# Loading one input in longer packets, reordering a kernel's opening, and holding back its weights

## The chip, the cores and the metric

One core of one Trainium2 chip. The metric is the device time of one execution in microseconds (us). Medians and means are over several runs, and every run is listed with the clock that TensorE (PE) was granted on average. A run of this one-core program is labelled "slow" when it is over 1.5% above the fastest run of the same kernel in the same call; verdicts use "fast" runs alone. That label matters here and I come back to it.

## The reference, cut to what matters

A Mamba-2 scan over 4 batches, 8 heads and 768 tokens, then an MLP with a hard-swish between two products:

```
# scan, by chunks
M = (C @ B.T) * exp(cum_i - cum_j) * causal
y = M @ x + (C @ state) * exp(cum_i)
state = exp(sum(la)) * state + sum_j(B_j x_j * exp(cum_last - cum_j))
# MLP on the transposed scan output
h = x @ w_in            # 3072x256 by 256x2048, weights come as float64
g = h * clip(h + 3, 0, 6) / 6
out = g @ w_out
```

## The kernel before

It works in 6 chunks of 128 tokens for all 4 batches. The scan of chunk 0 must be finished before the first product `h` can start. The weights arrive as float64 and are decoded to fp32 on VectorE and ScalarE, in 8 blocks of 1 MB (4 of w_in, 4 of w_out); block 0 is loaded at the start, block 1 is needed at the ninth product of h (the fifth f). The parts that the change touches (cuts are marked):

```
def load_bc(c):
    ...
    if c < TURN:                                    # TURN = 3
        bcs[c] = [tokens_first(C, name="C", tag="bc")]   # one transfer, 64-byte packets
    Bs[c] = tokens_first(B, name="B")
    ...
def load_w(i, hold=False):
    raw = loads.tile([P, NK * FP * 2 * P], U32, name="raw", bufs=NRAW)
    if hold:
        nc.gpsimd.memset(raw[:, :1], 0)             # queued on GpSimd behind ends()
    ...
    nc.sync.dma_start(out=dst, in_=src)

def decode(i):                                      # a generator; weights(i, n) takes n steps
    nc.scalar.copy(out=s, in_=top)
    ...
    if i == 1:
        next(parts_m); next(parts_m)                # significand, two VectorE steps, first
    yield
    # we and ws on VectorE; yield; exponent on ScalarE; yield; exponent again; yield
    # last two VectorE steps: we | ws, then w_in (or w_out) = m * e

# the opening
    diff(0, *range(NB)); store_rows()
    weights(0, 2); diff_exp(0, 0); diff_exp(0, 1); weights(0, 1)
    diff_exp(0, 2); diff_exp(0, 3); weights(0, 1)
    first_eto(); diff(1, 2, 3)
    for b in range(NB):
        ends(0, b)                                  # bs = B * L, on GpSimd
    load_w(1, hold=True); load_w(2); load_w(3)
    t_ps = turn_ps(0, 0)
    turn_c(0, t_ps)                                 # C turned on PE, into PSUM
    diff(1, 0, 1); busy(1, ...); turn_cum(c_ps); weights(0, 1)
    turn_b(0); by_token(c_ps); fade_c(0, t_ps)
    diff_exp(1, 2); diff_exp(1, 3)
    scores(0); multiply(0); renew(0); mix(0); keep(0)
    weights(1, 5)
```

`scores` makes cb = C B^T and the new state's products (y), `multiply` multiplies the decays L by cb in four VectorE steps, `mix` makes y, `keep` copies it out.

## Time and profile before

| | before |
|---|---|
| median (3 runs, then 4) | 365.87 us, then 365.69 us |
| profiled run | 366.87 us, span 365.2 us, mean granted clock 0.986 |
| first h | 27.36 us |
| decode of block 1 starts on VectorE | 27.75 us |
| first o (second product) | 57.25 us |

The profile's lines for this are in the prediction below. To read them: PE and PEld are the matmuls and weight loads of TensorE, DVE is VectorE, ACT ScalarE, POOL GpSimd and SPq the queue of SyncE, which issues the transfers (DMA); "issue" is time in which an engine waited for nothing that the profile shows, and the clock row of the page is in tenths of full speed.

### The profile page before, as it was taken

The numbers are of one execution on the slowest core, as the hardware profiler recorded it, in microseconds if no ns is written. First come the engines' busy times: TensorE is split into PE (matmuls) and PEld (weight loads), VectorE is DVE, ScalarE is ACT, GpSimd is POOL, SyncE is SP. The second block draws the span as 40 slices with busy tenths as digits, with TensorE's granted clock in tenths as the row PEclk, the third lists the DMA queues.
The fourth block names the chain that finished last, engine by engine and source line by source line (L and its number), as shares of the span: only waits on it lengthen the run. The fifth ranks groups of instructions, "written<-read, shape, count | busy, mean of one in ns | idle before, by whom it ended". The sixth has DMA issues, their size and how long they took to land.

```text
span 365.2 us, 9345 instructions
## 1 busy us (share of the span) xinstructions
PE 352.7 (97%) x3938; PEld 302.1 (83%) x3938; DVE 225.1 (62%) x427; ACT 177.0 (48%) x389; POOL 138.5 (38%) x139
## 2 busy tenths in 40 slices
PE   6859999999999999999999999999999999999996
PEld 2644447888788999888999888999888999888996
DVE  6637999989588626488436488436488421488111
ACT  3626887458557380366380366380366110376100
POOL 3300000084188922059922059820057800058800
PEclk9967999999999999999999999999999999999999
DMA  8986959910945016442016442000000000000000
GB/s 162 111 334 165 115 211 174 175 29 31 187 57 75 5 44 135 66 86 23 2 31 148 67 83 25 2 4 31 29 2 1 2 4 31 30 3 0 2 29 31
DMA packets 78538, 24.97 MB, mean 68 GB/s; under 512 B 69088, under 2 KB 74880, under 8 KB 77984
## 3 DMA queue, kind: packets, MB, share of 16 engines
q1 hardware_dynamic: 78496, 24.37, 34.4%
q8 instruction: 31, 0.51, 0.6%
q14 instruction: 11, 0.09, 0.1%
HBM read 21.07 MB, written 3.29 MB: 67 GB/s over the span
## 4 chain that ended last, share of the span: by engine, by line
PE 91%; DVE 4%; issue 2%; ACT 1%; DMA 1%; DVEq 0%; ACTq 0%
PE ob L749 18%; PE even L638 18%; PE oa L749 17%; PE odd L638 13%; PE h L596 8%; PE o L690 8%; PE y L571 3%; PE y L483 2%; PE cb L505 2%; PE y L517 1%; DVE cT L433 1%; PE d L340 1%; PE d L349 1%; ACT even L653 1%; DMA pre<-in_a_dram 1%
## 5 line engine op out<-in xcount | busy, mean ns | idle before, releaser
L735 POOL TENSOR_TENSOR s<-gT 128x512 f32<-128x512 f32 x20 | 26.4, 1321 | 91.4 <-DVE gT L679 91.4
L638 PE MATMUL even<-ts,w_sum 128*128 128x256 f32 x160 | 48.2, 383 | 0.0
L653 ACT COPY even<-odd 128x512 f32<-128x512 f32 x40 | 23.0, 576 | 48.9 <-PE odd L638 46.7
L674 ACT ACTIVATE gT<-odd,half 128x512 f32<-128x512 f32 x40 | 27.5, 687 | 35.0 <-DVE odd L667 35.0
L638 PE MATMUL odd<-yT,w_in 128*128 128x256 f32 x160 | 41.1, 379 | 0.0
L749 PE MATMUL oa<-w_out,gT 128*128 128x128 f32 x320 | 38.9, 277 | 0.0
L749 PEld LDWEIGHTS oa<-w_out,gT 128*128 128x128 f32 x320 | 38.1, 192 | 0.9
L749 PE MATMUL ob<-w_out,s 128*128 128x128 f32 x320 | 37.4, 275 | 0.0
L749 PEld LDWEIGHTS ob<-w_out,s 128*128 128x128 f32 x320 | 36.5, 192 | 0.0
L638 PEld LDWEIGHTS even<-ts,w_sum 128*128 128x128 f32 x160 | 29.9, 190 | 5.3 <-ACT up L660 1.5
L679 DVE SCALAR_TENSOR_TENSOR gT<-gT,odd 128x512 f32<-128x512 f32 x40 | 27.5, 688 | 9.9 <-ACT gT L674 9.9
L638 PEld LDWEIGHTS odd<-yT,w_in 128*128 128x128 f32 x160 | 30.1, 190 | 3.9
L377 ACT ACTIVATE L<-L,cum_n 128x64 f32<-128x64 f32 x128 | 31.1, 335 | 0.0
L749 PE MATMUL ob<-t,gT 128*128 128x128 f32 x240 | 30.3, 279 | 0.0
L596 PE MATMUL h<-yT,w_in 128*128 128x512 f32 x64 | 30.0, 632 | 0.0
L679 DVE SCALAR_TENSOR_TENSOR gT<-gT,even 128x512 f32<-128x512 f32 x40 | 27.2, 679 | 4.4 <-ACT gT L674 4.4
L674 ACT ACTIVATE gT<-even,half 128x512 f32<-128x512 f32 x40 | 27.8, 694 | 4.4 <-PE even L638 4.4
L654 DVE COPY up<-odd 128x256 f32<-128x256 f32 x40 | 17.0, 425 | 19.3 <-ACT even L653 18.6
L749 PEld LDWEIGHTS ob<-t,gT 128*128 128x128 f32 x240 | 27.9, 192 | 1.1 <-issue 0.4
L690 PE MATMUL o<-w_out,gT 128*128 128x256 f32 x128 | 28.5, 381 | 0.0
L395 POOL TENSOR_TENSOR tmp<-state,eto 128x256 f32<-128x256 f32 x5 | 3.2, 637 | 65.0 <-ACT eto L381 64.9
L690 PEld LDWEIGHTS o<-w_out,gT 128*128 128x128 f32 x128 | 24.1, 190 | 3.7 <-issue 0.5
(129 smaller groups left out, 629.7 us busy)
## 6 DMA issues: line engine op xcount, KB each, us to landing
raw<-in_moe_w_in_dram SPq DMA_DIRECT2D x4, 1024.0 KB
raw<-in_moe_w_out_dram SPq DMA_DIRECT2D x4, 1024.0 KB
L<-cum_d SPq DMA_DIRECT2D x8, 512.0 KB
xt<-in_x_dram SPq DMA_DIRECT2D x6, 512.0 KB
out_dram<-res SPq DMA_DIRECT2D x20, 128.0 KB
B<-in_B_dram SPq DMA_DIRECT2D x6, 256.0 KB
eto<-cum_e SPq DMA_DIRECT2D x20, 64.0 KB
C<-in_C_dram SPq DMA_DIRECT2D x3, 256.0 KB
```

The costliest lines, as they stand in the source:

```text
L377: nc.scalar.activation(Ls[c][:, b, h], Ls[c][:, b, h], AF.Exp, bias=cum_n[:, c, g:g + 1])
L483: nc.tensor.matmul(out=ys[c][a, q // 2][d0:d0 + 2 * D, b], lhsT=state[pair, b], rhs=csT[pair, b, HALF[a]], start=(a == 0 and b == 0), stop ...
L571: nc.tensor.matmul(out=ys[c][a, u][d0:d0 + D, b], lhsT=xt[rows, b * NH + h], rhs=Ls[c][rows, b, h], start=(b == 0 and a >= min(c, 1)), sto ...
L596: nc.tensor.matmul(out=h.rearrange("p r i -> p (r i)"), lhsT=w_in[:, j, f * P:(f + 1) * P], rhs=yTs[k][:, j].rearrange("p b i -> p (b i)") ...
L638: nc.tensor.matmul(out=bank[:, r], lhsT=lhsT, rhs=rhs, start=start, stop=True, skip_group_check=True)
L653: nc.scalar.copy(out=even, in_=odd[:, 1:2].to_broadcast([P, 2, 2 * P]))
L654: nc.vector.tensor_copy(out=up[:, 1], in_=odd[:, 0])
L674: nc.scalar.activation(gTs[k][:, f], h.rearrange("p r i -> p (r i)"), AF.Relu, bias=half, scale=1.0 / 6.0)
L679: nc.vector.scalar_tensor_tensor(out=g, in0=g, scalar=1.0, in1=h.rearrange("p r i -> p (r i)"), op0=ALU.min, op1=ALU.mult)
L690: nc.tensor.matmul(out=o[:, b % 2], lhsT=gTs[0][:, f, b * P:(b + 1) * P], rhs=w_out[:, f], start=(f == 0 and b % 2 == 0), stop=True, skip_ ...
L735: nc.gpsimd.tensor_tensor(out=o, in0=p_, in1=q_, op=op)
L749: nc.tensor.matmul(out=bank[:, slot], lhsT=lhs[:, j], rhs=rhs[:, j], start=(clear and j == 0), stop=True, skip_group_check=True)
```

## The change

The intent: C of chunk 0 comes in longer packets and is turned by VectorE, which frees PE and PSUM; the opening of all engines is put in another order; and the three weight transfers are held until VectorE has done its second multiplication, so that they do not sit in front of what the scan still needs. The core of the diff (small helpers and renamed banks cut):

```
-        if c < TURN:
+        if c == 0:
+            bcs[c] = [pairs_first(C)]              # 8 transfers, 256-byte packets
+        elif c < TURN:
             bcs[c] = [tokens_first(C, name="C", tag="bc")]
...
-        if hold:
-            nc.gpsimd.memset(raw[:, :1], 0)
+        if behind is not None:
+            nc.gpsimd.tensor_copy(raw[:, :1].bitcast(FP32), behind)
...
-        if i == 1:
+        if i < 2:                                  # significand first, block 0 too
...
+    for b in range(2):
+        mask_again(0, b)
+    diff(0, 0, 1)
+    diff(0, 2, 3)
+    turn_squares(bcs[0][0], turned(0)[2])          # transpose on VectorE
+    part_heads(0)                                  # cT from SBUF
+    for b in range(NB):
+        diff_exp(0, b)
+    first_eto()
+    weights(0, 1)
     add_up(ends_at[1])
     store_rows()
     diff(1, 2, 3)
+    turn_b(0)
     for b in range(NB):
         ends(0, b)
+    weights(0, 1)
+    diff(1, 0, 1)
+    diff_exp(1, 2)
+    diff_exp(1, 3)
+    weights(0, 2)
+    scores(0)
+    multiply(0)
+    load_w(1, behind=Ls[0][:, 0, 2, :1])           # after the second multiplication
     load_w(2)
     load_w(3)
+    c_ps = ...; turn_cum(c_ps); by_token(c_ps); busy(1, ...)
+    fade(0, HALF[1])
     weights(0, 1)
     mix(0)
     keep(0)
-    weights(1, 5)
+    weights(1, 2)
+    renew(0)
+    weights(1, 3)
```

More of the change, by code (lines that the diff above doesn't have):

```diff
@@ L123, with load_w @@
     raws = {}
-    def load_w(i, hold=False):
+    def load_w(i, behind=None):
         raw = loads.tile([P, NK * FP * 2 * P], U32, name="raw", bufs=NRAW)
-        if hold:
-            nc.gpsimd.memset(raw[:, :1], 0)
+        if behind is not None:
+            nc.gpsimd.tensor_copy(raw[:, :1].bitcast(FP32), behind)
         if i < NP:
@@ L337, in diff_mask, with mask_again @@
         ds[c, b] = d
+    def mask_again(c, b):
+        nc.tensor.matmul(
+            out=ds[c, b], lhsT=ident_h, rhs=hide.unsqueeze(1).to_broadcast([P, NH, HT]),
+            start=True, stop=True)
     def diff_less(c, b):
@@ L359, in first_eto @@
     def first_eto():
-        e_ps = ps.tile([P, NB, HT], FP32, name="e_ps", tag="f1")
+        e_ps = ps.tile([P, NB, HT], FP32, name="e_ps", tag="f0")
         for b in range(NB):
@@ L408, in turn_ps @@
         if c < 2:
-            return ps.tile([P, NB, P], FP32, name="t_ps", tag=f"f{2 * j}")
+            return ps.tile([P, NB, P], FP32, name="t_ps", tag=f"f{2 * j if c else 1}")
         return ps_o.tile([P, NB, P], FP32, name="t_ps", tag="o")
@@ L437, in fade_c @@
     def fade_c(c, t_ps):
-        sl = slice(0, P) if c else HALF[1]
-        nc.vector.tensor_tensor(
-            out=turned(c)[2][:, :, sl], in0=t_ps[:, :, sl], in1=etos[c][:, :, sl], op=ALU.mult)
+        nc.vector.tensor_tensor(out=turned(c)[2], in0=t_ps, in1=etos[c], op=ALU.mult)
     def turn(c, j):
@@ L455, in wake, with turn_squares, part_heads @@
             ends(c, b)
-    def turn_all(c):
-        bT, cT, csT = turned(c)
-        for t, out_ in zip(bcs[c], (csT, bT)):
-            nc.vector.transpose(
-                out=out_.rearrange("r b (s a) -> r b a s", a=4),
-                in_=t.rearrange("s t b a n -> s (b a) t n"))
+    def turn_squares(t, out):
+        nc.vector.transpose(
+            out=out.rearrange("r b (s a) -> r b a s", a=4),
+            in_=t.rearrange("s t b a n -> s (b a) t n"))
+    def part_heads(c):
+        _, cT, csT = turned(c)
         for t in range(2):
@@ L467, in turn_all, with fade @@
                 op0=ALU.mult)
-        nc.vector.tensor_tensor(out=csT, in0=csT, in1=etos[c], op=ALU.mult)
+    def fade(c, sl=slice(0, P)):
+        csT = turned(c)[2][:, :, sl]
+        nc.vector.tensor_tensor(out=csT, in0=csT, in1=etos[c][:, :, sl], op=ALU.mult)
+    def turn_all(c):
+        bT, _, csT = turned(c)
+        for t, out_ in zip(bcs[c], (csT, bT)):
+            turn_squares(t, out_)
+        part_heads(c)
+        fade(c)
     def busy(n, bank):
@@ L584, in keep @@
             y, dst = ys[c][a, u], yTs[c][:, u, :, HALF[a]]
-            if c == 0 and a and u:
-                nc.vector.tensor_copy(dst, y)
-            else:
-                nc.scalar.copy(out=dst, in_=y)
+            nc.scalar.copy(out=dst, in_=y)
     gTs, outs = {}, {}
@@ L840 @@
     in_three()
+    for b in range(2):
[8 more added lines that the diff above has]
+    weights(0, 1)
     add_up(ends_at[1])
-    diff(0, *range(NB))
     store_rows()
-    weights(0, 2)
-    diff_exp(0, 0)
-    diff_exp(0, 1)
-    weights(0, 1)
-    diff_exp(0, 2)
-    diff_exp(0, 3)
-    weights(0, 1)
-    first_eto()
     diff(1, 2, 3)
+    turn_b(0)
     for b in range(NB):
         ends(0, b)
-    load_w(1, hold=True)
+    weights(0, 1)
[6 more added lines that the diff above has]
+    load_w(1, behind=Ls[0][:, 0, 2, :1])
     load_w(2)
     load_w(3)
-    t_ps = turn_ps(0, 0)
-    turn_c(0, t_ps)
-    diff(1, 0, 1)
-    busy(1, ps.tile([P, NB * P], FP32, name="d", tag="f3"))
-    c_ps = ps.tile([P, NC, G], FP32, name="c_ps", tag="f3")
+    c_ps = ps.tile([P, NC, G], FP32, name="c_ps", tag="f1")
     turn_cum(c_ps)
+    by_token(c_ps)
+    busy(1, ps.tile([P, NB * P], FP32, name="d", tag="f0"))
+    fade(0, HALF[1])
     weights(0, 1)
-    turn_b(0)
-    by_token(c_ps)
-    fade_c(0, t_ps)
-    diff_exp(1, 2)
-    diff_exp(1, 3)
-    scores(0)
-    multiply(0)
-    renew(0)
     mix(0)
     keep(0)
-    weights(1, 5)
+    weights(1, 2)
+    renew(0)
+    weights(1, 3)
     load_eto(1)
```

## The prediction

> **What bounds the kernel now.** I first read the page: busy table, slices, chain.
>
> ```profile
> span 365.2 us, 9345 instructions
> PE 352.7 (97%) x3938; PEld 302.1 (83%) x3938; DVE 225.1 (62%) x427; ACT 177.0 (48%) x389; POOL 138.5 (38%) x139
> PE   6859999999999999999999999999999999999996
> PEclk9967999999999999999999999999999999999999
> ```
>
> The multiplying engine (PE) is the bound from slice 4 to the end. Only slices 1 to 3 (27 us) are not full, and the PE clock is low in slices 3 and 4. The change edits this opening only; from the first matmul of h on, instructions are the same. So the question is how much earlier h starts, at which clock it starts, and whether the decoded weights arrive as much earlier.
>
> The chain of waits, cut to the opening (start us, us, what), then the timeline of the same stretch:
>
> ```profile
> 12.64 1.41 DVE cT L433 x2
> 14.05 0.61 DVE we L226
> 14.68 1.32 DVE w_in L234
> 16.68 1.20 PE cb L505 x60
> 20.02 3.71 issue
> 24.16 1.04 PE y L483 x16
> 27.36 29.89 PE h L596 x64
> ```
>
> ```profile
> 19.12 0.90 PE L571 MATMUL y<-L,xt 64*32 64x64 f32 x59 [0.46 <-ACT adds L533]
> 23.73 0.43 PE L571 MATMUL y<-L,xt 64*32 64x64 f32 x5 [3.71 <-issue]
> ```
>
> Two things are to be seen. VectorE decodes weight block 0 (we, w_in) ahead of csT, and the first scores (cb) wait for csT, because they reuse its PSUM bank. And PE stops for 3.71 us in the middle of 64 like matmuls, with no semaphore to wait for. I counted PE's instructions: about 700 of the trace precede the stop[...]. The raw records of the instruction queue show 16 KB fetches beginning at 11.1, 21.2 and 25.9 us. [...] the three 1 MB weight transfers, issued at 16.33, send their first packets at 17.0. PE resumes 1.4 us after that fetch lands. So I read the stop as a fetch queued behind weights.
>
> The stretches (us, busy of PE, PEld, DVE, ACT, POOL, PEclk, DMA share, GB/s) show the clock:
>
> ```profile
> 11.30:21.57 10.27, 7.31 (x268) 5.22 (x268) 7.29 (x13) 4.55 (x10) 2.99 (x5) 1.00 0.92 206
> 21.57:31.80 10.23, 8.07 (x107) 4.91 (x107) 3.02 (x5) 3.73 (x6) 0.00 (x0) 0.50 0.46 182
> 31.80:57.25 25.45, 25.45 (x61) 11.34 (x60) 23.61 (x35) 21.32 (x28) 0.00 (x0) 1.00 0.86 192
> ```
>
> At half clock until 31.80, the first h matmuls are 0.853 us apart instead of 0.429. From 27.36 to 31.80 that loses 4.44 / 2 = 2.2 us. In the third row VectorE is busy 23.61 of 25.45 us: the decode has little room there.
>
> [...] cT from t_ps takes 745 ns, from csT in SBUF 478.
>
> **The change part by part.**
>
> *C in packets of 256 bytes.* Before, C is 4096 packets of 64 bytes, moving from 5.5 to about 8 us by the raw records, landed at 10.45. It becomes 8 transfers with 1024 packets in all. Issue costs 8 x 0.54 us (these transfers' issue in later chunks) instead of 0.46. By the order view, the eighth waits for the semaphore that weight block 0 releases; that lands at 7.33. With 1.9 us from issue to landing (cum_d: 14.79 to 16.71), C is there at 9.4, 1 us sooner. B is issued only after it, at 7.9, and so lands at 13.2 to 13.7 (before 13.17); x lands at 16.2 to 16.6 (before 16.24). These two do not gain.
>
> *Turn on VectorE.* It adds a transpose of 1.10 us and two scalings of 0.48 and removes two of 0.745 and four PE transposes (0.60 us). VectorE: 9.4 + 1.10 + 0.96 = 11.5; significand of block 0, 0.69 + 1.23, makes 13.4; the long scan 1.21 makes 14.65; we and ws 0.86 make 15.5. It is then free for the multiplications by cb; only two block-0 steps (0.69 + 1.3) remain, behind those.
>
> *PE's opening.* Two repeated masks fill an idle gap. Decays in two halves: 6.47 + 2 x 1.8 = 10.1; e_ps 0.33; two decays of chunk 1, 1.5: 11.95. It waits for B until 13.5; transposes 0.6: 14.1; bT on ScalarE 0.58: 14.7; the other decays 1.2: 15.3. So cb starts at 15.3 to 15.6, not 16.68, a gain of 1.2. cb 1.2 and state 0.8: 17.4, just behind x. Four multiplications of 0.62: 16.6 to 19.1; cum_n 0.26 and fade 0.42: 19.8. ScalarE, with two decode steps of 1.16 in front, copies adds by 18.5. The first mix runs from 18.6 to 19.6, then waits for the fade; 1.05 + 1.1 + 1.05 from 19.8 gives h at **23.0**. That is 4.36 earlier: 3.71 from the removed stop, only 0.65 from everything else.
>
> *Weights held.* They wait for the second multiplication, 17.8, and are issued at about 18.05 instead of 16.33. [...] Block 1 lands at 21.56 + 1.72 = 23.3. Significand to 25.3, we and ws to 26.2, ScalarE's two steps to 28.1 (renew fills that wait), then 0.69 + 1.23: w_in block 1 is ready at 30.1, before 34.47: 4.35 earlier. Block 0 is ready at 21.8, in time.
>
> *The sum.* At full clock PE would want block 1 at 23.0 + 8 x 0.858 = 29.9, and the bank that gT frees at 30.7: a wait of 0.8 us. The tightest later need is w_out block 0, ready before at 56.56 for a start at 57.25: 0.69 us of slack. So the VectorE chain allows at most 4.35 + 0.69 = **5.0** us. If h starts at half clock as before, PE itself gains 4.36 and the slack stays. From slice 7 on nothing changes. Gain 4.4 to 5.0; 365.9 - 4.7 = **361.2 us**.
>
> **Rivals.** (1) *The fetch is still late, or the next one is.* For: [...] the weights still come within 2 us of it. Against: the fetch is asked for first. A residual of 1 to 3 us gives 362.5 to 364.5. (2) *A wait takes the place of the stop*: B, x or the eighth C transfer. For: B's issue now waits for weight block 0, and PE idles 1.5 us for B. If B and x slip by 1.5 us more, h starts 1.5 later: 362.7. (3) *The late weights bound it.* If VectorE's decode cannot follow, the gain falls to 3 to 4: 362 to 363. For: 23.61 busy of 25.45. Against: block 1 formerly lay landed for 5 us (21.56 to 26.61) before ScalarE took it. (4) *More than I count.* Without the stop the clock may never fall; 2.2 us more would make 359, yet the VectorE chain stands against most of it. (5) *The stop is no fetch*: then it stays, and only 0.7 us are won, 365.2.
>
> **Range and chances.** Main case (65%): 360.5 to 362. Rivals 1 to 3 together 22%, up to 364.5; rival 4 8%, down to 358.7; rival 5 5%. So 8 in 10 lie between 359.4 and 363.8. Over 2% faster is below 358.6, which needs more than 7.3 us: 0.06. Slower by 2% needs +7.3 us; nothing shows that: 0.02. Within 2%: 0.92.
>
> **What would show it.** Right: no PE gap of "issue" above 1 us in the first mix; a 16 KB fetch between 16 and 18.5 us, ahead of weight packets; cb from about 15.4; h from about 23.0; weights issued near 18; the transpose of C starting at about 9.4; a stream from 90 us on that looks as before, shifted by 4 to 5 us. Wrong: h starting after 24.5 (then see which of B, x or fetch); h early but PE waiting for VectorE more than 1.5 us between h start and the first o (weights too late); or a clock that falls later, in the middle of h.

## The result, and the profile after

The changed kernel takes 363.82 us in the median (363.45 to 364.41, 4 runs) against 365.69 (365.42 to 366.42, 4 runs). The ratio is 0.9947, interval 0.9926 to 0.9969: within 2%, a gain of 1.9 us, where 4.7 were predicted. Ratios here are the mean time of one kernel's fast runs over that of the other's in the same rounds, so not quite the ratio of the medians.

The page of the changed kernel, its span, busy line and clock:

```profile
span 361.9 us, 9354 instructions
PE 349.9 (97%) x3936; PEld 300.7 (83%) x3936; DVE 225.7 (62%) x427; ACT 177.4 (49%) x390; POOL 140.5 (39%) x139
PEclk9699999999999999999999999999999999999999
```

The two profiles differ by 3.3 us, more than the medians do: the profiled run of before (366.87) was one of its slower ones, that of after (363.57) one of its faster. By the label of the later calls, in which runs of before above about 366 us count as slow, that run would be slow. So what is read from its profile alone is checked below on runs labelled fast; the stop of PE, for one, is seen in those of e2 and e12.

The timeline of the changed kernel's PE (start us, us, engine, line, operation; in brackets the idle time before it and what ended it):

```profile
13.34 1.09 PE L423 MATMUL t_ps<-ident,B 128*128 128x128 f32 x4 [3.20 <-DMA B<-in_B_dram]
16.20 2.01 PE L523 MATMUL cb<-cT,bT 32*64 32x128 f32 x64
21.10 0.97 PE L589 MATMUL y<-L,xt 64*32 64x64 f32 x64
24.00 7.13 PE L611 MATMUL h<-yT,w_in 128*128 128x512 f32 x16
32.47 3.70 PE L611 MATMUL h<-yT,w_in 128*128 128x512 f32 x8 [1.33 <-DVE gT L694]
```

The first mix (L589) is whole: the stop of 3.71 us is gone. h starts at 24.00 instead of 27.30 (the same view; 27.36 in the chain of waits) and at full speed, 16 matmuls in 7.13 us. Then a new wait appears: PE stands for 1.33 us ahead of the ninth product, for VectorE. In all it waits 1.7 us between 24.00 and the first o (30.10 less 28.41 busy, below).

The stretches (us, busy of PE, PEld, DVE, ACT, POOL, PEclk, DMA share, GB/s) show where the half clock went (PEclk 0.50):

```profile
12.32:19.15 6.83, 5.81 (x166) 4.49 (x166) 5.93 (x9) 3.70 (x5) 3.88 (x4) 0.50 0.75 101
24.00:54.10 30.10, 28.41 (x69) 11.90 (x65) 26.74 (x41) 24.15 (x31) 0.00 (x0) 1.00 0.99 232
```

It now covers the wait for B's aftermath: t_ps, the decays of chunk 1 and cb (2.01 us for what took 1.20 before). The chain of waits of the changed kernel (start us, us, what) runs through the weights:

```profile
8.05 5.15 DMA B<-in_B_dram
16.28 2.06 PE cb L523 x64
18.34 1.30 DVE L L564 x2
19.91 5.18 DMA raw<-in_moe_w_in_dram
25.11 0.70 DVE wm L202
31.74 1.28 DVE gT L694 x2
46.98 7.13 PE h L611 x16
```

B lands, PE turns it and makes cb, VectorE does two multiplications, only then are the weights asked for (19.91), they land 5.2 us later, and from 25.11 on the decode holds PE. VectorE's own line shows how much of this was the wait for cb, 0.83 us:

```profile
18.34 2.48 DVE L564 TENSOR_TENSOR L<-L,cb 128x512 f32<-128x512 f32 x4 [0.83 <-PE cb L523]
```

Before, the decode started later, but for another reason. This is VectorE's timeline of the kernel before:

```profile
27.41 0.42 DVE L586 COPY yT<-y 128x256 f32<-128x256 f32 x1 [6.01 <-PE y L483]
27.75 0.68 DVE L199 TENSOR_SCALAR wm<-raw 128x1024 uint32<-128x1024 uint32 x1
```

There it waited for PE, while the block had landed at 21.6. So the decode begins 27.75 - 25.11 = 2.64 us earlier. The first o comes at 46.98 + 7.13 = 54.11 instead of 57.25, 3.14 earlier, and from there to the end nothing changes (307.9 and 307.8 us).

### The profile page after: what moved, and what is told of

Read it like the earlier page. It is cut to its first block, busy times and chain, and to the rows that moved or that the text cites. A ratio compares the mean times of both kernels' runs of the same rounds, so it can differ in the third digit from the quotient of the medians.

```text
span 361.9 us, 9354 instructions
## 1 busy us (share of the span) xinstructions
PE 349.9 (97%) x3936; PEld 300.7 (83%) x3936; DVE 225.7 (62%) x427; ACT 177.4 (49%) x390; POOL 140.5 (39%) x139
## 4 chain that ended last, share of the span: by engine, by line
PE 81%; DVE 6%; SPq 5%; DMA 4%; ACT 2%; issue 1%; POOL 0%; DVEq 0%; ACTq 0%
PE ob L764 18%; PE oa L764 17%; PE even L653 16%; PE odd L653 12%; PE o L705 8%; SPq L100 4%; PE cb L523 2%; PE y L589 2%; PE h L611 2%; PE y L501 2%; DVE gT L694 2%; DMA raw<-in_moe_w_in_dram 1%; DMA B<-in_B_dram 1%; PE y L535 1%; DVE wm L206 1%; ACT we L222 1%
## 5 line engine op out<-in xcount | busy, mean ns | idle before, releaser
L611 PE MATMUL h<-yT,w_in 128*128 128x512 f32 x64 | 28.4, 599 | 1.7 <-DVE gT L694 1.3
L159 POOL TENSOR_SCALAR_AFFINE_SELECT L<-L 64x1024 f32<-64x1024 f32 (+1 forms) x16 | 20.2, 1266 | 17.3 <-DMA L<-cum_d 16.9
```

The lines of the kernel that those rows point to most:

```text
L159: nc.gpsimd.affine_select(out=t[rows], in_=t[rows], pattern=pattern, compare_op=ALU.is_ge, fill=-1e5, base=base, channel_multiplier=-1)
L611: nc.tensor.matmul(out=h.rearrange("p r i -> p (r i)"), lhsT=w_in[:, j, f * P:(f + 1) * P], rhs=yTs[k][:, j].rearrange("p b i -> p (b i)") ...
```

## The experiments

Twelve kernels in three calls of four, 5 rounds each; the calls ran on three different chips. All gave correct results, and all their runs but three (of e12) were labelled fast. Means are over all runs.

| label | kernel | runs | mean | median | ratio to before, 95% |
|---|---|---|---|---|---|
| e1_hold_fourth | changed, hold on 4th multiplication | 22 | 365.38 | 365.26 | 1.0053 (1.0024 to 1.0083) |
| e2_hold_as_before | changed, old hold | 13 | 362.90 | 362.43 | 0.9924 (0.9890 to 0.9957) |
| e3_before_with_hold | before, new hold only | 6 | 362.53 | 362.75 | 0.9896 (0.9860 to 0.9932) |
| e4_c_64_bytes | changed, C as before | 6 | 362.76 | 362.67 | 0.9903 (0.9872 to 0.9934) |
| e5_after_again | changed | 22 | 363.90 | 363.92 | 0.9973 (0.9948 to 0.9997) |
| e6_fill_wait | changed, wait for B filled | 22 | 363.22 | 363.26 | 0.9951 (0.9930 to 0.9971) |
| e7_c_64_hold_first | e4, hold on 1st multiplication | 22 | 362.65 | 362.45 | 0.9932 (0.9909 to 0.9955) |
| e8_before_hold_first | e3, hold on 1st multiplication | 17 | 362.44 | 362.19 | 0.9967 (0.9930 to 1.0004) |
| e9_exponent_sooner | changed, one decode step moved | 6 | 363.29 | 363.24 | 0.9922 (0.9907 to 0.9937) |
| e10_c_64_first_exponent | e7 with that step | 5 | 362.18 | 362.03 | 0.9892 (0.9874 to 0.9910) |
| e11_before_first_exponent | e8 with that step | 6 | 361.63 | 361.90 | 0.9877 (0.9854 to 0.9900) |
| e12_before_shift32 | before, 32 more PE instructions | 13 | 363.95 | 363.81 | 0.9938 (0.9892 to 0.9985) |

**The kernel before is itself spread.** It ran 122 times beside these, 360.48 to 367.53 us. By mean granted clock: 6 runs at 1.0, median 360.8; 10 at 0.994 to 0.995, median 362.7; 55 at 0.989 to 0.991, median 365.8; 51 at 0.984 to 0.986, median 366.6. As the fastest runs are near 360.5, the label calls everything above 366 slow: 16 of 34, 45 of 70 and 8 of 18 runs. The ratios above leave those out, so they understate what the changes do to the usual run, and they are not comparable from one call to another: the runs of before that count as fast average 363.8, 363.9 and 365.2 in the three calls. I therefore compare the kernels of one call with each other by their own means, and say where a comparison crosses calls. What these low-clock runs have in common is seen in only one profile of this kernel; no profile of one of its six best runs was taken. These six (360.48 to 361.37) beat every one of the 26 timed runs of the changed kernel (362.81 at best): the change makes the usual run of this kernel faster, but not its best one.

### e1: is it the landing of the weights that sets the end?

```
-    load_w(1, behind=Ls[0][:, 0, 2, :1])
+    load_w(1, behind=Ls[0][:, 0, 6, :1])
```

> The changed kernel with its weights held until the fourth multiplication by cb instead of the second (two multiplications of 0.62 us later, so the issue moves from 19.91 to about 21.15 us). Theory A (the decode of weight block 1 on VectorE, started by the landing of that block, sets when the first matmuls on all blocks end): about 1.2 us slower than the changed kernel, near 365.0. Theory B (PE's own start of h sets it, and the late weights hide in slack): no difference, 363.8.

365.38 against 363.90 for the changed kernel (e5, another call): 1.5 slower for 1.24 us of delay. Across calls, theory A holds in direction and roughly in size, and nothing speaks for the late weights hiding in slack.

The profiles say the same more sharply. This is the start of the decode of block 1 on VectorE, and the first o by the chain of waits, for each kernel with this decode:

| | decode starts | first o | difference |
|---|---|---|---|
| changed | 25.11 | 54.11 | 29.00 |
| e5 | 25.95 | 54.95 | 29.00 |
| e3 | 24.25 | 53.27 | 29.02 |
| e4 | 23.84 | 52.84 | 29.00 |
| e6 | 24.75 | 53.76 | 29.01 |
| e7 | 23.33 | 52.33 | 29.00 |
| e8 | 23.08 | 52.09 | 29.01 |
| e1 | 25.39 | 55.08 | 29.69 |
| before | 27.75 | 57.25 | 29.50 |
| e12 | 23.92 | 53.07 | 29.15 |
| e2 | 24.16 | 54.12 | 29.96 |

In seven profiles the time to the first o is one constant, whatever PE did: h started at 22.4 in e3 and at 24.9 in e5. Three exceptions are those in which PE ran part of h at half clock and so was the bound itself (before until 31.8; e12 until 27.3; e1 from 32.3 to 35.7 us). The fourth is e2: there ScalarE came late to its part of the decode, at 25.89, behind the stop of PE and the last copy of yT. So the landing of the weights sets the end only as long as PE and ScalarE keep up. e9 to e11, whose decode is shortened, have 28.35, 28.33 and 28.24.

### e2 and e3: what the hold gives and takes

e2 gives the changed kernel the old hold:

```
-    load_w(1, behind=Ls[0][:, 0, 2, :1])
+    load_w(1, hold=True)                 # memset on GpSimd, behind ends()
```

> The changed kernel with the old hold (a memset behind the four products on GpSimd, which end at 17.2 us), so weights are issued about 2.5 us earlier, near 17.3. Theory A with the fetch theory: the 16 KB instruction fetch that began at 18.69 us falls behind the weights' first packets and a stop of 1 to 4 us with no releaser comes back in the first mix, but the decode starts 2.5 us earlier; as the decode is the bound, the total gets faster by 1 to 2.5 us in spite of the stop unless the stop exceeds the slack of PE (about 1.3 us). If the stop is no instruction fetch: no stop, 2 to 2.5 us faster, near 361.5.

Mean 362.90, median 362.43: the hold as written costs the changed kernel about 1 us (across calls). The profiled run of e2 (363.51) shows no such gain: its first o comes at 54.12, that of the changed kernel at 54.11. PE's timeline of e2:

```profile
21.33 0.95 PE L591 MATMUL y<-L,xt 64*32 64x64 f32 x62
23.27 0.30 PE L591 MATMUL y<-L,xt 64*32 64x64 f32 x2 [0.99 <-issue]
```

The stop is back, shorter. The weights were issued at 17.93 instead of 19.91, their first packets moved at 18.97, and the 16 KB fetch began at 20.97. In the changed kernel and in e3 it began 0.35 us after the end of cb; here cb ended at 18.56. Its runs spread from 361.6 to 366.9.

e3 gives the kernel before the new hold and nothing else:

```
-    load_w(1, hold=True); load_w(2); load_w(3)      # ahead of turn_c
...
     multiply(0)
+    load_w(1, behind=Ls[0][:, 0, 2, :1]); load_w(2); load_w(3)
```

> The kernel before with only the new hold. Fetch theory: the stop of 3.71 us in the first mix is gone, h starts near 23.7 us; weights issued near 19.4, block 1 lands near 24.6, so by theory A the decode starts 3.1 us earlier than before (27.75) and the total is 2 to 3 us faster than before, so as fast as the whole change or faster. Rival (the new order and the C load carry the gain): less than 0.7 us faster than before.

362.53 on average (6 runs, five at a clock of 1.0), against 365.18 for all 34 runs of before in that call, and ratio 0.9896 to its fast ones. **The hold alone is worth as much as the whole change or more**; the rival, that order and C carry the gain, is refuted. PE's timeline of e3:

```profile
18.75 0.90 PE L571 MATMUL y<-L,xt 64*32 64x64 f32 x59 [0.46 <-ACT adds L533]
20.20 0.30 PE L571 MATMUL y<-L,xt 64*32 64x64 f32 x5 [0.56 <-issue]
```

0.56 us of the 3.71 are left; the fetch began at 17.90 (21.23 before), ahead of the weights, whose first packets moved at 20.17.

### e4: does the new C load help?

```
-        if c == 0:
-            bcs[c] = [pairs_first(C)]
-        elif c < TURN:
+        if c < TURN:
...
-    turn_squares(bcs[0][0], turned(0)[2]); part_heads(0)
...
     diff(1, 2, 3)
+    c_turned = ps.tile([P, NB, P], FP32, name="t_ps", tag="f2")
+    turn_c(0, c_turned)                  # on PE; csT faded at once
```

> The changed kernel (its order and its hold kept) with C of chunk 0 loaded in one transfer of 64-byte packets and turned on PE as before. Theory C (eight issues of 0.57 us each cost more than the longer packets save, and put B later): B lands earlier by 0.1 to 0.6 us, cb, hold and decode follow, total 0 to 1 us faster than the changed kernel. Rival (the new C load is what gains): 1 us or more slower than the changed kernel, because PE and VectorE have the PSUM turn again.

362.76, 1.1 us less than the changed kernel (e5, another call). The new load, together with the turn on VectorE that belongs to it, is a loss. SyncE's timeline of the changed kernel, then of before:

```profile
1.73 6.28 SPq L100 DMA_DIRECT2D pairs<-in_C_dram  x8
8.05 0.47 SPq L93 DMA_DIRECT2D B<-in_B_dram  x1
```

```profile
1.74 0.46 SPq L92 DMA_DIRECT2D C<-in_C_dram  x1
2.24 5.55 SPq L92 DMA_DIRECT2D B<-in_B_dram  x1
```

The eight small transfers keep SyncE for 6.28 us: seven take 0.53 to 0.71 us each, the fifth 2.06. In the records of packets C moves at some 137 packets of 256 bytes per 0.5 us, 70 GB/s, and less after 7.5 us, and is through at 10.0; as one transfer of 64-byte packets it moved at about 1000 to 1100 per 0.5 us, 128 to 141 GB/s, and all but the last few were through by 8, the last at 8.4. The pace of issue is not what held the first half up: four transfers had been issued by 4.18 us, their packets began at 5.41, and with all four at hand they still took 0.46 us each, one after another. From 6.0 to 7.5 us the 16 DMA engines were busy to a share of 0.31 to 0.32, where before it was over 1 (1.47 to 1.61, as packets overlap): by the records of packets some 5 were in flight on average, against 24 to 25 before. The records give each small transfer four landings and the single transfer sixteen, so each small one seems to have used a quarter of the engines; that is inferred, no experiment varied it. C landed at 11.09 (10.45 before), and VectorE's first use of it is at 11.17 us, where I had 9.4:

```profile
11.17 1.08 DVE L466 STREAM_TRANSPOSE csT<-pairs 128x512 f32<-128x512 f32 x1 [4.76 <-DMA pairs<-in_C_dram]
```

In e4, C is turned on PE from 10.19, B is there at 12.65 instead of 13.34, cb runs at full clock (1.21 us) from 14.29, and the weights are issued at 18.44.

### e5 and e6: what the half clock costs

e5 is the changed kernel once more.

> The changed kernel once more, unchanged, as the reference of this call and for more runs of it with their clocks. Expected 363.4 to 364.4 as before. Theory D (the 1.8 us by which the weights were released later than I predicted come from the half clock between 12.3 and 19.2 us, after PE waited 3.2 us for B): runs whose clock did not fall in that stretch are faster by up to 1.7 us, so the times spread over 362 to 364.5 with the mean clock of the run as a rough guide.

363.90 on average, 22 runs from 362.81 to 364.90. By clock: ten at 0.991, median 364.2; ten at 0.995, median 363.9. The spread is there, but the two groups lie 0.3 us apart, where I expected up to 1.7; the one run at 0.998 is the fastest, 362.81.

e6 fills PE's wait for B:

```
     diff(1, 2, 3)
+    busy(3, ps.tile([P, NB * P], FP32, name="d", tag="f2"))
     turn_b(0)
```

> The changed kernel with three idle matmuls of 128x512 fp32 (about 2.6 us at full clock) in PE's wait for B. Theory D: the clock stays up through t_ps, the decays of chunk 1 and cb; cb takes 1.2 us and not 2.06, the weights are released near 18.0 instead of 19.91, the decode of block 1 starts near 23.3 instead of 25.11, and the total falls by 1 to 1.8 us, to about 362.3. Rival (the wait for B alone sets the release, the clock drop is beside it): no difference beyond 0.3 us.

363.22 against 363.90 in the same call, both 22 runs: **0.7 us faster**, not 1.0 to 1.8. The clock is kept up (15 of 22 runs at 1.0, in e5 none), and cb takes 1.21 us in its profile. So here filling the wait for B kept the clock up more often and gained 0.7 us, but a second limit lies close behind. That the clock alone makes the 0.7 is not shown: within e6 the 15 runs at 1.0 are no faster (mean 363.29) than the other seven (363.08). The chain of waits of e6:

```profile
14.61 3.14 POOL bs L397 x4
17.78 1.30 DVE L L564 x2
19.34 5.38 DMA raw<-in_moe_w_in_dram
24.75 0.70 DVE wm L202
```

The multiplications overwrite L, and the products bs on GpSimd read L, so they must be done first; bs itself waits for B. In this run B came late (14.47). e1's profile separates the limits better: up to this point it is the changed kernel, C and B landed at 11.05 and 13.28 (11.09 and 13.21 there), PE waited 3.21 us for B (3.20 there), and yet the clock stayed full (cb took 1.21 us there, 2.01 in the changed kernel). A wait of this length thus need not lower the clock. Where the clock fell to half, it fell 1.5 us after PE had stopped in the kernel before (stopped at 20.02, low from 21.57 to 31.81), 2.2 us after in the changed kernel (10.13, low from 12.32 to 19.15), 2.1 us after in e12 (18.33, low from 20.43 to 27.26) and 2.1 us after in the later part of e1 (30.17, low from 32.3 to 35.7). In e1 cb ended early, and VectorE's own work up to ws, behind C's late landing, was the last to finish: the multiplications began at 17.39 instead of 18.34. Three things end within about a microsecond: cb at half clock (18.3), bs (17.2 to 17.8), VectorE's chain behind C (17.4).

### e7, e8: the hold on the first multiplication

```
-    load_w(1, behind=Ls[0][:, 0, 2, :1])
+    load_w(1, behind=Ls[0][:, 0, 0, :1])
```

In e7 it is applied to e4, in e8 to e3.

> The kernel of e4 (C in 64-byte packets, new order) with the weights held until the first multiplication, 0.62 us sooner. Theory A: 0.5 to 0.6 us faster than e4, near 362.1. Fetch theory: the fetch begins at about 17.5 us and the first weight packets come about 1.5 us after the first multiplication, so no stop over 1 us comes back.

> The kernel before with only the new hold, but on the first multiplication: weights issued at about 18.5 instead of 19.13 (e3). Theory A: 0.5 to 0.6 us faster than e3, near 362.1, with clocks of 0.995 or 1.0 in nearly all runs because the stop stays short. If the fetch is caught behind the weights again: a stop of over 1 us in the first mix and a wide spread of times as of the kernel before.

362.65 and 362.44, so 0.1 less than e4 and e3, where 0.5 to 0.6 were expected, and those ran in another call: inconclusive by time. The profiles show the decode 0.5 us (e4 to e7) and 1.2 us (e3 to e8) earlier, but other steps of the opening also moved, and the stop in e8 is 1.20 us:

```profile
19.69 0.31 PE L571 MATMUL y<-L,xt 64*32 64x64 f32 x5 [1.20 <-issue]
```

The weights' packets do not explain this one: the fetch ran from 17.31 to 18.34, and the weights' first packet moved at 18.34. So a stop of 0.56 to 1.20 us is left at this place even with the fetch ahead of the weights (e3, e11 with 0.71, e8). Against e5, of the same call, e7 is 1.25 us and e8 1.46 us faster.

### e9 to e11: shorten the decode itself

```
-        if i < 2:
-            next(parts_m)
-            next(parts_m)
+        if i == 0:
+            next(parts_m)
+            next(parts_m)
+        elif i == 1:                      # the second significand step comes behind we, ws
+            next(parts_m)
```

> The changed kernel, with one VectorE step of the decode of block 1 moved: the second step of the significand (1.23 us) comes behind we and ws instead of ahead of them, so ScalarE's two exponent steps can start about 0.75 us sooner. Theory A (from the landing of block 1 to w_in the decode is a serial chain that sets the total): 0.6 to 0.8 us faster than the changed kernel of the last call (363.9), near 363.2. If the start of h or the DMA sets the total: no difference.

> e7 (C in 64-byte packets, new order, hold on the first multiplication) with the same moved step. Theory A: 0.5 to 0.8 us faster than e7 (mean 362.65), near 361.9; PE's wait ahead of the ninth product of h nearly gone.

> e8 (the kernel before with the hold on the first multiplication) with the same moved step. Theory A: 0.5 to 0.8 us faster than e8 (mean 362.44), near 361.7.

363.29, 362.18 and 361.63: 0.6 less than e5, 0.5 less than e7, 0.8 less than e8, each time across calls, each time in the expected direction and about the expected size. (Of e8 and e11 the runs at a clock of 1.0 alone give 362.14 and 361.63, so 0.5.) Within the profiles nothing crosses: from the landing of block 1 to the first multiplication by gT takes 31.74 - 25.11 = 6.63 us in the changed kernel, and 31.34 - 25.36 = 5.98 in e9. PE's wait ahead of the ninth product is gone in e10, and in e9 half of what it was:

```profile
32.08 4.13 PE L613 MATMUL h<-yT,w_in 128*128 128x512 f32 x9 [0.66 <-DVE gT L696]
```

e11, which is the kernel before with the hold on the first multiplication and this step, is the fastest kernel of the study on average: 361.63 (360.27 to 362.83), all six runs at a clock of 1.0. It keeps the old C load and the old order.

### e12: is the stop a fetch of instructions?

```
             d = ps.tile([P, NH, HT], FP32, name="d", tag=f"f{b}")
+            for _ in range(16 if b == 0 else 0):
+                nc.tensor.matmul(
+                    out=d[:, 0, :1], lhsT=ident_h, rhs=ident_h[:, :1], start=True, stop=True)
```

> The kernel before with 32 more instructions on PE (16 weight loads and 16 matmuls of one column) in its idle time at the start, no other change. Fetch theory: the stop in the first mix [...] moves 32 instructions forward, from after about 59 of the 64 matmuls to after about 43 to 45; the total stays within 1 us of before. If the stop is tied to data (an operand, a bank) and not to the count of instructions, it stays after matmul 59.

PE's timeline of e12:

```profile
17.65 0.67 PE L574 MATMUL y<-L,xt 64*32 64x64 f32 x43 [0.46 <-ACT adds L536]
19.98 0.42 PE L574 MATMUL y<-L,xt 64*32 64x64 f32 x21 [1.65 <-issue]
```

The stop moved from behind matmul 59 to behind matmul 43, that is by 16 pairs, exactly the 32 instructions that were put in ahead. It belongs to the count of instructions and to nothing that those matmuls read or write. The fetch of this run began at 16.58, as the weights' first packets moved (16.61), and took 2.32 us, against 0.92 to 1.40 in the eleven profiles in which it went ahead of them. The time is spread as that of before (361.4 to 367.5); its five runs at a clock of 1.0 have a median of 361.4.

## Why the prediction was wrong

The range, 359.4 to 363.8, was missed by a hair at its upper end; the gain was two fifths of what I forecast. By the prediction's own steps:

- **The stop is a fetch behind the weights: right as far as the runs show.** It shrank from 3.71 to 0.56 us with the hold (e3), came back when the weights went out 2 us sooner (e2, 0.99 us), and moved by 32 instructions when 32 were put in (e12). When the fetch was asked for, no record shows; that it queued is my inference from its start, at 21.23 us behind the weights' first packets (17.37) and at 17.90 ahead of them (20.17, e3). Up to 1.20 us of it can remain with the fetch ahead of the weights (e8). Two small readings were off: the weights' first packets moved at 17.37, not 17.0, and PE resumed 1.5 us after the fetch landed, not 1.4.
- **h starts at 23.0: a microsecond off.** Measured 24.00, at full clock.
- **C is there at 9.4: wrong.** It landed at 11.09. The issues kept my time, though the one that stood was the fifth: the eighth began at 7.48, and B was issued at 8.05 where I had 7.9. What failed is the 1.9 us from issue to landing, which I had taken from another transfer (cum_d). It was 3.6 us, as the eight transfers moved at 70 GB/s. e4 shows the old load and turn to be better by 1.1 us, all effects together.
- **B at 13.2 to 13.7: right** (13.34). That PE idles for it I had seen; that the clock fell to 0.50 beside it, from 12.32 to 19.15 us in the profile, I had not drawn in.
- **"cb 1.2" and the decays before it, at full-clock durations: the step that failed.** Together with t_ps they took 5.0 us (13.34 to 18.34) instead of the 3.0 that I gave them (13.5 to 16.5). So the second multiplication ended at 19.64, not at 17.8, and the weights were issued at 19.91, not at 18.05. I priced the half clock for h alone. It is half of the error: VectorE waited 0.83 us for cb, and at full clock, as in e1's profile, the multiplications begin at 17.39, 0.95 us sooner. The other 0.9 of the 1.84 us is VectorE's work behind the late C, which ends at 17.4 and not at 15.5 as in my sum. e6 agrees, with a gain of 0.7; bs, which its multiplications waited for, was not in my sum.
- **Block 1 lands at 23.3, decode 4.35 us earlier: wrong by what it inherited.** The 5.25 us from issue to landing in my sum were right (5.18). Measured: 25.11, and 2.64 earlier.
- **The sum: the rule was right, the term mis-sized.** I wrote that the VectorE chain allows at most its own shift plus 0.69 us of slack. With the measured 2.64 that makes 3.33; the first o came 3.14 earlier, and the two spans differ by 3.3. Rival 3, "the late weights bound it", at a gain of 3 to 4, is what the profile shows, and so is my sign of it, PE waiting for VectorE more than 1.5 us between h and the first o (1.7).
- **The baseline: a second miss.** I subtracted from the median a gain worked out from one profile. That profile's run took 366.87 us, 1.2 above the median of 365.69. The two profiled runs differ by 3.30 us, the medians by 1.87. I had seen its half clock during h and took it for the kernel's usual course. That was not wrong (106 of the 122 later runs have a mean clock of 0.991 or less), but the runs lie up to 7 us apart, and this one was among the slowest.

What stays open: how often the kernel before is spared the drop of the clock, and whether the stop is short in its fastest runs. It fits that the variants of before with a shorter stop (e3, e8, e11: 0.56 to 1.20 us) have a clock of 1.0 in 23 of 29 runs, and before in 6 of 122, but a profile of such a run of before was not taken; and kernels without a stop have it less often (e4 and e7 in 7 of 28 runs). The split of the late release, about half to the clock and half to C, rests on two profiled runs.

## What to carry to other kernels

A hold that keeps a bulk transfer out of the way of something small has a price, the start of everything that waits for the bulk (in e1 1.24 us more of it cost 1.5 us, across calls); find out which of the two ends last before placing it, and hold only as long as the small thing needs. When a long packet is bought with many more transfers, look at what they move together, not only at the count of packets: here 3072 fewer packets took longer, because the eight small transfers moved at about half the rate of the single one (70 against 128 to 141 GB/s). And price PE's work in an opening at the clock that profiles show there (0.50 for 6.83 us in the changed kernel, after PE had begun a wait of 3.20 us), and take the baseline from many runs when the clock varies.
